# Every fourth column of wo and w2 per result column, and a store of 128 runs of 8 bytes without the turn

## The chip, the core and the metric

The kernel runs on one core of a Trainium2 chip. Its engines are TensorE (PE; PEld is its loading of weights), VectorE (DVE), ScalarE (ACT), GpSimd (POOL) and SyncE (SP), with 16 DMA engines. SBUF is the on-chip memory with 128 partitions, PSUM the memory that TensorE writes to. The metric is device time in microseconds (us), the median of several executions.

## What is computed

One token goes through two branches, which a gate mixes:

```
q = x @ wq                                  # 32 heads of 128
p = softmax(q . k * 128**-0.5)              # each head over 4096 cached keys
a = concat(p . v) @ wo                      # 4096 -> 512
b = relu(x @ w1 + b1)**2 @ w2 + b2          # 512 -> 1376 -> 512
g = sigmoid(sum(x * gate_w))
out = g * a + (1 - g) * b                   # 512 values, bf16
```

All inputs are bf16. The caches of keys and values are 32 MB each; wq and wo are 4 MB each, w1 and w2 1.4 MB each. Every byte is used once.

## The kernel before

**Stages.** The 32 heads are worked in 8 groups of 4 (`NQ`, `R`). For each group a block of keys (K, 4 MB) and of values (V, 4 MB) is loaded. Part of the key scores is computed on DVE (L680, L684), the rest by turning keys on TensorE (L455), copying them on ACT (L350) and multiplying (L462). Then come the softmax (L367 on ACT) and the product with V (`pv`, L492 and L496). The engines run side by side and hand over by semaphores; TensorE's program is a loop written with branches.

**The order of the loads** is written out by hand (`ORDER`, L59): SP issues wq, then K and V blocks, each after the block that held its buffer is done (`done`, L243). w1 is issued behind the third block, once `s_z` and `s_b2` are up (L268, L269). wo comes in four parts of 1 MB; a part goes out when the earlier one in its buffer has been used (`s_wd`, L254). w2 comes last, in five pieces (`W2_PARTS`, L65): 4, 4, the rest of 96 rows, 1 and 1 blocks of 128 rows. Small inputs are loaded on ACT's queue at the start: x, gate_w, b1 and b2 (L321 to L324).

**The output sum.** `acc` is 128 partitions by 4 columns of fp32 in PSUM. It takes all products of both branches: `out_rows` (L524) adds 32 products for each of four groups of rows of wo, `mlp_out` (L533) 4 products for each block of w2. In column j, `acc` holds the values 128j to 128j + 127, since the weights of a product are 128 consecutive columns of wo or w2. The bias b2 is brought to that layout near the start: it is loaded as 4 rows of 128, turned by one transpose on TensorE (L603) into `B2`, and multiplied with 1 - g on DVE (`bias`, L668).

**The end.** TensorE runs `out_rows(1)`, then the five pieces of `mlp_out`, each behind the wait for its load. DVE adds the bias and casts to bf16 (`accs`, L751). TensorE turns the 128 x 4 sum into 4 x 128 (L641), DVE copies it to SBUF (`fin4`, L753), and SP stores it as 4 runs of 256 bytes (L281). SP waits for that store behind a barrier of all engines (L755, L756).

Of the kernel before, what the change touches and what calls it, by code (L numbers as in the profile page):

```python
# [5 lines left out]
def bass_gated_mix__gqa_block_cached__dense_activation_squared_relu__decode_kernel(  # L6
# [16 lines left out]
    bf16 = mybir.dt.bfloat16  # L23
# [6 lines left out]
    DM = 512  # L30
# [49 lines left out]
    with ctx:  # L80
        def sb(name, shape, dt):
            return ctx.enter_context(nc.sbuf_tensor(name, shape, dt))

        def pb(name, shape, dt):
            return ctx.enter_context(nc.psum_tensor(name, shape, dt))

        def sem(name):
            return ctx.enter_context(nc.semaphore(name))
# [5 lines left out]
        wo_sb = W[:, 0:2 * TB * DM].rearrange("p (g t n) -> p g t n", g=2, t=TB)  # L94
# [4 lines left out]
        w1_sb = sb("w1_sb", [128, 4, F], bf16)  # L99
# [7 lines left out]
        xrow = w1_sb[0:1, 0, 0:DM]  # L107
        grow = w1_sb[0:1, 1, 0:DM]
        b1r = sb("b1r", [1, F], bf16)
        b2r = w1_sb[0:4, 2, 0:128]  # L110
        oT = sb("oT", [GH, 128], bf16)
        o2 = sb("o2", [128, TB], bf16)
        fin4 = sb("fin4", [4, 128], bf16)
        zeros = sb("zeros", [128, 128], bf16)
        xb = sb("xb", [128, 4, 128], bf16)
        ident = sb("ident", [128, 128], bf16)
# [19 lines left out]
        hs = sb("hs", [128, FG + 1], bf16)  # L136
        b2g = sb("b2g", [128, 4], fp32)
        accs = sb("accs", [128, 4], bf16)
# [4 lines left out]
        pO = pb("pO", [128, 512], fp32)  # L143
# [6 lines left out]
        OT = KP[2][0:GH, 0:128]  # L150
        O2 = KP[3][:, 0:2 * TB].bitcast(fp32)
        Z = pO[:, 76:77]
        B2 = pO[:, 78:80].bitcast(bf16)
        acc4 = pO[0:4, 128:192].bitcast(bf16)
        QR = [pQ[:, :]] + [p[:, :].bitcast(fp32) for p in KP[0:3]] + [pQ[:, :]] * (NQ - QF)
        H = KP[0][:, 0:2 * (FG + 1)].bitcast(fp32)
        acc = pQ[:, 256:260]
# [3 lines left out]
        s_b = sem("s_b")  # L161
# [20 lines left out]
        s_b2 = sem("s_b2")  # L182
# [27 lines left out]
        s_oc = sem("s_oc")  # L210
        s_acc = sem("s_acc")
        s_as = sem("s_as")
        s_fin = sem("s_fin")
        s_f4 = sem("s_f4")
        s_out = sem("s_out")

        def key(q, b):
# [10 lines left out]
        @block.sync  # L228
        def _(eng):
            def load_kv(n):  # L230
                kind, q = ORDER[n]
                if q >= 2:
                    done(kind, q - 2)
                if kind == "K":
                    eng.dma_start(KV[:, K_SLOT[q], :], k_q[q, :, :]).then_inc(s_k[q], 16)
                else:
                    at = 0
                    for m, sv in zip(V_PARTS[q], s_v[q]):
                        a, b = at * PB * 128, (at + m) * PB * 128
                        eng.dma_start(KV[:, V_SLOT[q], a:b], v_q[q, :, a:b]).then_inc(sv, 16)  # L240
                        at += m

            def done(kind, q):  # L243
                if kind == "K":
                    eng.wait_ge(s_sd, NP * (q + 1))
                    eng.wait_ge(s_t, GQ * (q + 1))
                else:
                    eng.wait_ge(s_pv, q + 1)

            def load_wo(g):  # L250
                if g == 0:
                    eng.wait_ge(s_qps, NQ)
                elif g < NG - 1:
                    eng.wait_ge(s_wd, g)  # L254
                a = 0 if g < NG - 1 else 1
                eng.dma_start(wo_sb[:, a, :, :], wo_v[g, :, :, :]).then_inc(s_wo[a], 16)  # L256

            def load_w2(n):
                a, b = W2_PARTS[n]
                if a < FG:  # L260
                    eng.dma_start(w2a[:, a:b, :], w2_v[:, a:b, :]).then_inc(s_w2[n], 16)  # L261
                else:
                    eng.dma_start(w2b[:, :], B_w2[FG * 128:F, :]).then_inc(s_w2[n], 16)

            for n in range(len(ORDER)):
                load_kv(n)
                if n == 2:
                    eng.wait_ge(s_z, 1)  # L268
                    eng.wait_ge(s_b2, 1)  # L269
                    eng.dma_start(w1_sb[:, :, :], w1_v[:, :, :]).then_inc(s_w1, 16)  # L270
                if n in WO_AT:
                    load_wo(WO_AT[n])
            load_wo(NG - 1)
            eng.wait_ge(s_sd, NP * NQ)
            load_w2(0)
            load_w2(1)
            load_w2(2)
            load_w2(3)
            load_w2(4)
            eng.wait_ge(s_f4, 1)  # L280
            eng.dma_start(out[0, 0, :].rearrange("(j p) -> j p", p=128), fin4[:, :]).then_inc(s_out, 16)  # L281


        @block.gpsimd
# [35 lines left out]
        def _(eng):  # L320
            eng.dma_start(xrow, A_x[0, :, :]).then_inc(s_x, 16)  # L321
            eng.dma_start(grow, gate_w.rearrange("(a n) -> a n", a=1)).then_inc(s_gw, 16)
            eng.dma_start(b1r[:, :], B_b1.rearrange("(a n) -> a n", a=1)).then_inc(s_b, 16)
            eng.dma_start(b2r, B_b2.rearrange("(j p) -> j p", p=128)).then_inc(s_b, 16)  # L324
            eng.wait_ge(s_xc, 1)
            eng.activation(xcolf[:, :], XC, ACT.Copy).then_inc(s_xf, 1)
            eng.wait_ge(s_xf, 1)
# [75 lines left out]
        def _(eng):  # L403
# [45 lines left out]
            def take(sm, n=1):  # L449
                eng.wait_ge(sm, n).then_inc(sm, -n)  # L450
# [73 lines left out]
            def out_rows(a):  # L524
                take(s_oc)
                take(s_wo[a], 16)
                for t in range(TB):
                    for j in range(4):
                        mm = eng.matmul(acc[:, j:j + 1], wo_sb[:, a, t, j * 128:(j + 1) * 128], o2[:, t:t + 1],
                                        start=False, stop=False, skip_group_check=True)  # L530
                mm.then_inc(s_wd, 1)

            def mlp_out(c, last=False):  # L533
                eng.wait_ge(s_w2[c], 16)
                a, b = W2_PARTS[c]
                for n in range(a, b):
                    M = 128 if n < FG else FR
                    w = w2a[:, n, :] if n < FG else w2b[:, :]
                    for j in range(4):
                        mm = eng.matmul(acc[:, j:j + 1], w[:, j * 128:(j + 1) * 128], hs[0:M, n:n + 1],  # L540
                                        start=False, stop=last, skip_group_check=True)
                if last:
                    mm.then_inc(s_acc, 1)
# [33 lines left out]

            at("rows")
            out_rows(0)
            branch("IS_GE", LAST, "next", "rows2")  # L580
            at("rows2")
# [6 lines left out]
            for t in range(4):  # L588
                mm = eng.matmul(XC[:, t:t + 1], xrow[:, t:DM:4], ident[0:1, 0:1], start=True, stop=True)
# [10 lines left out]
            eng.wait_ge(s_qc, QF)  # L600
            eng.wait_ge(s_b, 32)
            eng.wait_ge(s_ez, 1)
            eng.transpose(B2, b2r, ident[0:4, 0:4]).then_inc(s_b2, 1)  # L603

            part("k0")
            keys(0, extra[0])
# [24 lines left out]
            turn()  # L631
            spread()
            out_rows(1)
            eng.wait_ge(s_hs, 2)
            mlp_out(0)
            mlp_out(1)
            mlp_out(2)
            mlp_out(3)
            mlp_out(4, last=True)
            eng.wait_ge(s_as, 1)  # L640
            eng.transpose(acc4, accs[:, :], ident[:, :]).then_inc(s_fin, 1)  # L641


        @block.vector
        def _(eng):
# [20 lines left out]
            def bias():  # L666
                eng.wait_ge(s_b2, 1)
                eng.tensor_scalar(b2g[:, :], B2, omg[:, 0:1], None, ALU.mult).then_inc(s_bg, 1)  # L668

# [79 lines left out]
            eng.wait_ge(s_acc, 1)  # L749
            eng.wait_ge(s_bg, 1)  # L750
            eng.tensor_tensor(accs[:, :], acc[:, 0:4], b2g[:, :], ALU.add).then_inc(s_as, 1)  # L751
            eng.wait_ge(s_fin, 1)
            eng.tensor_copy(fin4[:, :], acc4).then_inc(s_f4, 1)  # L753

        body.close()  # L755
        nc.sync.wait_ge(s_out, 16)  # L756
# [28 lines left out]
```

## Time and profile before

| | |
|---|---|
| median of 3 executions (lowest, highest) | 190.78 us (190.7, 190.9) |
| the profiled execution's own time | 190.89 us |
| its span, first to last instruction | 189.40 us |
| mean granted TensorE clock | 0.732 |
| busy in the span: PE, PEld, DVE, ACT | 73%, 63%, 65%, 61% |
| HBM read | 78.32 MB, 414 GB/s over the span |

The span is cut into 40 slices of 4.7 us; in a row of tenths a 9 means that an engine was busy for 90% or more of the slice. A group of instructions is told by its line, engine and operation, then the tiles (out<-in) and the shapes (partitions x elements). The chain of waits goes back from the last instruction to whatever released it, step by step. SPq is the queue in which SP issues transfers. Times in the views count from the start of the span. The trace also holds records of single DMA packets and of semaphore changes, which the views sum up.

### The profile page before, as it was taken

How to read it: one execution, taken by the hardware profiler on the slowest of the kernel's cores; microseconds unless marked ns; L12 is line 12 of the kernel's file. 1: busy time of each engine (PE TensorE's matmuls, PEld its weight loads, DVE VectorE, ACT ScalarE, POOL GpSimd, SP SyncE). 2: the span in 40 equal slices, each digit the busy share in tenths (PEclk: the TensorE clock that was granted, in tenths of full speed). 3: DMA queues.
4: the chain of work that ended last, by engine and by line, in shares of the span. 5: the costliest groups of instructions: out<-in, count | busy, mean ns of one | idle time of the engine just before them, and what ended most of it. 6: DMA issues, size and time to landing. Idle time of an engine off the chain costs nothing. (4 is left out here: it accounts for less than half of the span.)

```text
span 189.4 us, 6230 instructions
## 1 busy us (share of the span) xinstructions
PE 137.5 (73%) x2685; PEld 119.8 (63%) x2688; DVE 122.7 (65%) x123; ACT 115.7 (61%) x242; POOL 6.0 (3%) x13
## 2 busy tenths in 40 slices
PE   0009496668839889969968797929867496899865
PEld 0003265546729689958858695919666585789854
DVE  1100199979959999996998299919990599701010
ACT  3004559949989985985987099708962298560000
POOL 4000000001600000000000000000000000000000
PEclk9999979979966965795885569555965588555555
DMA  6999999989989999999999999999999999999991
GB/s 225 437 443 443 443 443 439 422 365 484 433 379 438 429 443 439 431 429 429 443 431 401 436 429 436 443 443 429 417 448 408 422 431 434 445 398 410 424 382 68
DMA packets 4177, 78.47 MB, mean 414 GB/s; under 512 B 483, under 2 KB 837, under 8 KB 1094
## 3 DMA queue, kind: packets, MB, share of 16 engines
q1 hardware_dynamic: 4152, 78.32, 97.1%
q8 instruction: 7, 0.11, 0.2%
q14 instruction: 4, 0.03, 0.0%
q10 hardware_dynamic: 14, 0.01, 0.0%
HBM read 78.32 MB, written 0.00 MB: 414 GB/s over the span
## 5 line engine op out<-in xcount | busy, mean ns | idle before, releaser
L350 ACT ACTIVATE kT<-KP 128x1024 bf16<-128x1024 bf16 x80 | 75.2, 1043 | 25.8 <-PE KP L455 25.6
L680 DVE TENSOR_TENSOR w2a<-KV,qb 128x1536 f32<-128x1536 bf16 x32 | 56.1, 1752 | 19.1 <-DMA KV<-in_A_k_cache_dram 18.7
L455 PE MATMUL KP<-ident,KV 128*128 128x128 bf16 x640 | 58.3, 252 | 10.2 <-PEq L450 10.1
L684 DVE TENSOR_REDUCE S<-w2a 128x12 f32<-128x1536 f32 x32 | 56.1, 1753 | 1.1
L455 PEld LDWEIGHTS KP<-ident,KV 128*128 128x128 bf16 x640 | 47.2, 114 | 13.8 <-issue 12.8
L462 PE MATMUL pS<-qc,kT 128*128 128x4 bf16 x640 | 28.0, 165 | 13.2 <-PEq L450 11.2
L462 PEld LDWEIGHTS pS<-qc,kT 128*128 128x128 bf16 x640 | 24.4, 99 | 19.3 <-issue 18.0
L496 PEld LDWEIGHTS pO<-E,KV 128*128 128x128 bf16 x1024 | 29.4, 105 | 0.2 <-issue 0.2
L496 PE MATMUL pO<-E,KV 128*128 128x4 bf16 x1024 | 28.6, 166 | 0.1
L367 ACT ACTIVATE E<-S,nM 32x128 bf16<-32x128 f32 x32 | 18.5, 578 | 0.9
L440 PE MATMUL pQ<-W,xb 128*128 128x512 bf16 x17 | 6.7, 530 | 13.6 <-DMA W<-in_A_wq_dram 12.0
L333 ACT ACTIVATE qb<-pQ 32x128 bf16<-32x128 f32 x20 | 5.3, 268 | 13.9 <-PE pQ L440 13.5
L440 PEld LDWEIGHTS pQ<-W,xb 128*128 128x128 bf16 x20 | 2.2, 126 | 15.1 <-DMA W<-in_A_wq_dram 11.7
L356 ACT ACTIVATE S<-pS 32x80 f32<-32x80 f32 x32 | 7.3, 228 | 4.8 <-PE pS L462 4.2
L659 DVE TENSOR_SCALAR e<-ez 128x1 f32<-128x1 f32 x1 | 0.2, 155 | 13.7 <-ACT ez L382 13.7
L367 ACT ACTIVATION_READ_ACCUMULATOR E<-S,nM 32x1 f32 x32 | 8.1, 252 | 0.0
L703 DVE RECIPROCAL rden<-pO 128x4 f32<-128x4 f32 x8 | 1.4, 174 | 8.4 <-PE pO L496 8.4
L492 PE MATMUL pO<-RS,onesf 128*128 128x4 f32 x16 | 4.3, 340 | 1.4 <-PEq L450 1.4
L483 PE MATMUL pM<-identf,mp 128*1 128x128 f32 x8 | 2.9, 359 | 3.2 <-PEq L450 2.9
L492 PEld LDWEIGHTS pO<-RS,onesf 128*128 128x128 f32 x16 | 3.8, 298 | 1.7 <-issue 1.6
L487 PE MATMUL pM<-onesf,dg 1*128 1x1 f32 x16 | 4.1, 324 | 0.9 <-PEq L450 0.7
L440 PE MATMUL KP<-W,xb 128*128 128x512 bf16 x12 | 4.7, 576 | 0.0
(74 smaller groups left out, 68.9 us busy)
## 6 DMA issues: line engine op xcount, KB each, us to landing
KV<-in_A_k_cache_dram SPq DMA_DIRECT2D x8, 4096.0 KB, 21.9
KV<-in_A_v_cache_dram SPq DMA_DIRECT2D x7, 4096.0 KB, 29.5
W<-in_A_wq_dram SPq DMA_DIRECT2D x1, 4096.0 KB, 13.2
W<-in_A_wo_dram SPq DMA_DIRECT2D x4, 1024.0 KB, 16.7
KV<-in_A_v_cache_dram SPq DMA_DIRECT2D x1, 2048.0 KB, 11.3
KV<-in_A_v_cache_dram SPq DMA_DIRECT2D x2, 1024.0 KB, 14.3
w_sb<-in_B_w_dram SPq DMA_DIRECT2D x1, 1376.0 KB, 24.0
w2a<-in_B_w_dram SPq DMA_DIRECT2D x2, 512.0 KB, 18.8
```

What stands on the lines that cost most here:

```text
L333: eng.activation(qb[rows(r), c, :], QR[c][rows(r), r * 128:(r + 1) * 128], ACT.Copy)\
L350: eng.activation(kT[:, n % NT, :], KP[n % NKP][:, :], ACT.Copy).then_inc(s_ev, 1)
L356: eng.activation(S[rows(r), q % NS, 0:YQ], S2[rows(r), :, r], ACT.Copy).then_inc(s_cp, 1)
L367: eng.activation(E[rows(r), q % 2, :, r], S[rows(r), q % NS, :], ACT.Exp, bias=nM[rows(r), q:q + 1], scale=SCALE, accum_out=RS[rows(r), q ...
L440: mm = eng.matmul(QR[c], xb[:, t, :], wq_sb[:, t, c * 512:(c + 1) * 512], start=(t == 0), stop=(t == 3))
L455: mm = eng.transpose(KP[(GQ * a + g) % NKP][:, y * 128:(y + 1) * 128], key(a, b), ident[:, :])
L462: mm = eng.matmul(pS[:, R * c:R * c + R], kT[:, (GQ * a + g) % NT, y * 128:(y + 1) * 128], qc2[:, a, :], start=True, stop=True)
L487: eng.matmul(MB[:, a:a + 1], dg[:, a, :], onesf[0:1, 0:1], start=True, stop=True).then_inc(s_mb, 1)
L492: eng.matmul(DEN[a], onesf[:, :], RS[:, a, :], start=True, stop=True)
L496: mm = eng.matmul(O[a], KV[:, V_SLOT[a], b * 128:(b + 1) * 128], E[:, a, COLUMN[b], :], start=(b == 0), stop=(b == NB - 1))
L680: eng.tensor_tensor(prod, KV[:, K_SLOT[q], x:x + XB * 128].rearrange("p (b d) -> p b d", d=128), qb[:, q, :].unsqueeze(1).to_broadcast([12 ...
L684: eng.tensor_reduce(S[:, q % NS, c:c + XB], prod, AX.X, ALU.add).then_inc(s_sd, 1)
```

## The change

The weights of a product are no longer 128 consecutive columns but every fourth one, beginning at j. So column j of `acc` holds the values j, j + 4, j + 8 and so on, and partition p holds the four consecutive values 4p to 4p + 3. The turn (L641) and the copy (L753) are gone, with `fin4` and two semaphores. SP waits for the add and stores `accs` straight away, as 128 runs of 8 bytes. The bias follows the same layout: b2 is loaded as one row of 512, and four products with a 1 x 1 one, each reading every fourth element, put it into four fp32 columns of PSUM.

```diff
-        b2r = w1_sb[0:4, 2, 0:128]
+        b2r = w1_sb[0:1, 2, 0:DM]
...
-        B2 = pO[:, 78:80].bitcast(bf16)
-        acc4 = pO[0:4, 128:192].bitcast(bf16)
+        B2 = pO[:, 78:82]
...
-            eng.wait_ge(s_f4, 1)
-            eng.dma_start(out[0, 0, :].rearrange("(j p) -> j p", p=128), fin4[:, :]).then_inc(s_out, 16)
+            eng.wait_ge(s_as, 1)
+            eng.dma_start(out[0, 0, :].rearrange("(p j) -> p j", j=4), accs[:, :]).then_inc(s_out, 16)
...
-            eng.dma_start(b2r, B_b2.rearrange("(j p) -> j p", p=128)).then_inc(s_b, 16)
+            eng.dma_start(b2r, B_b2.rearrange("(a n) -> a n", a=1)).then_inc(s_b, 16)
...
-                        mm = eng.matmul(acc[:, j:j + 1], wo_sb[:, a, t, j * 128:(j + 1) * 128], o2[:, t:t + 1],
+                        mm = eng.matmul(acc[:, j:j + 1], wo_sb[:, a, t, j:DM:4], o2[:, t:t + 1],
...
-                        mm = eng.matmul(acc[:, j:j + 1], w[:, j * 128:(j + 1) * 128], hs[0:M, n:n + 1],
+                        mm = eng.matmul(acc[:, j:j + 1], w[:, j:DM:4], hs[0:M, n:n + 1],
...
-            eng.transpose(B2, b2r, ident[0:4, 0:4]).then_inc(s_b2, 1)
+            for j in range(4):
+                mm = eng.matmul(B2[:, j:j + 1], b2r[:, j:DM:4], ident[0:1, 0:1], start=True, stop=True)
+            mm.then_inc(s_b2, 1)
...
-            eng.wait_ge(s_as, 1)
-            eng.transpose(acc4, accs[:, :], ident[:, :]).then_inc(s_fin, 1)
...
-            eng.wait_ge(s_fin, 1)
-            eng.tensor_copy(fin4[:, :], acc4).then_inc(s_f4, 1)
```

More of the change, by code (lines that the diff above doesn't have):

```diff
@@ L109, in bass_gated_mix__gqa_block_cached__dense_activation_squared_relu__decode_kernel @@
         b1r = sb("b1r", [1, F], bf16)
-        b2r = w1_sb[0:4, 2, 0:128]
+        b2r = w1_sb[0:1, 2, 0:DM]
         oT = sb("oT", [GH, 128], bf16)
         o2 = sb("o2", [128, TB], bf16)
-        fin4 = sb("fin4", [4, 128], bf16)
         zeros = sb("zeros", [128, 128], bf16)
@@ L212, in bass_gated_mix__gqa_block_cached__dense_activation_squared_relu__decode_kernel @@
         s_as = sem("s_as")
-        s_fin = sem("s_fin")
-        s_f4 = sem("s_f4")
         s_out = sem("s_out")
```

## The prediction

> **What bounds the kernel now.** The page first: its second part shows the DMA engines full in nearly every slice, its third part puts the loading queue at 97.1% of them, and the weight loads of TensorE at 63%.
>
> ```profile
> DMA  6999999989989999999999999999999999999991
> ...
> q1 hardware_dynamic: 4152, 78.32, 97.1%
> ```
>
> So the 78 MB of loads set the time until they are in, and what the change does to compute before that matters only where compute holds back a load. After the last load comes a short tail in which nothing overlaps. The chain of waits, in order of time, shows both:
>
> ```profile
> 167.12 19.15 DMA w2a<-in_B_w_dram
> 186.26 0.05 issue
> 186.31 0.80 PE pQ L540 x24
> 187.11 0.03 issue
> 187.14 0.28 PE pQ L540 x4
> 187.42 0.02 issue
> 187.45 0.17 DVE accs L751
> 187.62 0.04 issue
> 187.66 0.28 PE pO L641
> 187.95 0.02 issue
> 187.97 0.21 DVE fin L753
> ```
>
> The reader is to see that the loads of w2 end at 186.3, and that then single instructions follow each other: the last w2 products, the add of the bias, the turn (L641), the copy (L753), and the store, which the chain no longer lists. The span ends at 189.40. One more thing is in the trace's semaphore records: the fifth piece of w2 lands at 187.09, so the last four products (187.14) wait for their own load, not for the 24 before them.
>
> The timeline of the last microseconds gives the store, and how densely products with consecutive columns stand:
>
> ```profile
> 185.34 0.50 PEld L540 LDWEIGHTS pQ<-hs,w2a 128*128 128x128 bf16 x16
> ...
> 188.21 0.33 SPq L281 DMA_DIRECT2D out_dram<-fin  x1
> ```
>
> Sixteen weight loads of 104 ns in 0.50 us: (0.50 - 0.104) / 15 = 26 to 27 ns from one to the next. I call this the step; it sets the rate of these products, each of which lasts 165 ns but overlaps the others.
>
> **What is removed.** The turn and the copy with their hand-overs. The add's semaphore is up at 187.620, the copy's at 188.193 (semaphore records), and SP issues 16 ns after it. SP would issue 16 ns after the add instead: 188.193 - 187.620 = **0.573 us** earlier. All of it lies on the path. In the built program of the changed kernel the store does wait for the add alone, so nothing else takes the place of the two. What is late next is the store itself; the engines' closing barrier is passed by 188.98, before the store's landing at 189.37, and moves with the issue.
>
> **Strided weights in the tail.** 76 products read every fourth column now: 32 of the last out_rows, 16 of the first piece of w2, 24 of the pieces two to four, and the last 4. Elements 8 bytes apart are loaded in one place of the trace (L589, one row, clock 1.00), elements 20 bytes apart in another (L508, clock 0.50; the last 4 of its 44 are consecutive):
>
> ```profile
> L589 PEld LDWEIGHTS pO<-ident,w_sb x4: 105/110/114, 2.1 to 2.2; 1*128 1x128 bf16 x4
> ...
> L508 PEld LDWEIGHTS KP<-xcol,w_sb x44: 136/157/196, 167.4 to 172.4; 128*128 128x128 bf16 x40, 128*96 128x96 bf16 x4
> ```
>
> L589's four fill 0.21 us, so its step is (0.21 - 0.11) / 3 = 32 ns against 27: 5 ns more. L508's starts stand 58 ns apart: 31 ns more. What hides it: the first 48 products start at 184.48 and the last of them starts at 185.74 (its load 185.739), while the second piece is waited for until 186.30, which leaves 0.54 us, or 11 ns each. The next 24 have until 187.14 instead of 186.95: 0.19 us, or 8 ns each. Only the last 4 pay whatever it is. At 32 ns a step that is 4 x 5 = 0.02 us. L589 ran at twice the clock of the tail; if its 5 ns become 10, the 24 overrun by 0.05 and the four add 0.04, together 0.09. I take **0.05**, between the two, because L589 has the same distance of bytes; the ends are 0 and, by L508's step, 76 x 58.5 = 4.45 us from 184.48, so a last step ending at 188.92 instead of 187.25: 1.68 us. A gain is excluded: the columns are no fewer.
>
> The Trainium skill (SBUF — State Buffer, "Door 1: The DMA port swizzle") says that memory is read at full rate as long as two accesses fall into one 16-byte line. By it the 8 bytes cost nothing and the sum below is 190.51 instead of 190.56; L508 at 20 bytes agrees with its other half, and no run here shows it at 128 rows and 8 bytes.
>
> **Strided weights earlier.** Three calls of out_rows (32 products each) become 0.16 us longer at 5 ns, 1.0 us at 31 ns. SP waits for them (L256) before it issues the next wo and the V behind it on its queue. The loads already issued cover that: the page has 21.9 us (K) and 29.5 us (V) from issue to landing, while 4096 KB at 443 GB/s need 9.5 us, so over 10 us are always queued. I cost it at nothing; without the cover it would be 0.16 us a call. At L603 four products replace one: 3 x 32 ns = 0.1 us later for s_b2. SP's wait there (L269) holds the load of w1, which lands 24.0 us after issue at 22.79 and is used at 167; TensorE itself then sits idle for 1.2 us until K0 is in (23.8). Nothing. The load of b2 as one run instead of four leaves the same queue before 2.1 us and is waited for at 22.4. The bias product (L668, 213 ns) reads fp32 now, like L751 (161 ns); it lies at 42.9, beside loads.
>
> **The store.** Now: 4 runs of 256 bytes. The packet records show issue at 188.209, packets on four DMA engines starting at 188.966 to 189.026 and taking 15 to 18 ns, and the last landing at 189.369, 0.32 us after the last packet. Then: 128 runs of 8 bytes. Packets of 8 bytes take 7 ns (one is in the trace) and the 4-byte ones after the store's data begin 12 ns behind them, so eight on an engine are some 8 x 12 = 0.10 us, 0.09 more than now. The only issue of 128 rows that met idle engines is the first (L223): issued at 0.740, it began on ten engines from 1.747 to 1.897, 17 ns apart, on four more until 2.292, on the last two at 2.706 and 2.780. At 17 ns sixteen engines begin within 15 x 17 = 0.25 us, 0.19 more than the store's 0.06 now. So +0.28; I take **0.30**, since ten of sixteen engines go that way. The ends: no cost (a gain of at most the 0.06 of spread), and the two late engines, (2.780 - 0.740) - (189.026 - 188.209) = 1.22, with the packets 1.31. SP's own 334 ns do not change: issues with 128 rows take 328.
>
> **The sum.** -0.573 + 0.05 + 0.30 = -0.22 us. The profiled execution took 190.89 (span 189.40 and 1.49 around it): 190.67. It lies 0.11 over the median 190.78, and against that the forecast is **190.56 us**. About 0.2% (0.38 us) is what a measurement of this kernel can tell from no change, so faster begins below 190.40 and slower above 191.16.
>
> **The rivals.**
>
> *The store costs almost nothing more.* If sixteen engines begin as close together as four do and the packets hide, it costs 0.05, the weights 0.02: -0.50, **190.28**. For it: the issue takes SP the same time, and the receipt (0.32 us) is the larger part. Against it: L223's spread. The Trainium skill (DMA: Bandwidth & Descriptors, "Anatomy of one DMA") holds that many descriptors can be emitted before their cost shows, which is this case. Chance 0.27.
>
> *Two engines begin late, as at L223*: -0.573 + 0.05 + 1.31 = +0.79, **191.57**. Against it: these were the kernel's first packets, and the two did it once. Chance 0.10.
>
> *The weight loads become the bound.* If 8 bytes cost what 20 do, TensorE is late by 1.68 us: -0.573 + 1.68 + 0.30 = +1.41, **192.19**. The place is the tail from 184.48 on; with the store at +0.30 the change loses once the last product is over 0.27 us late, at (187.25 + 0.27 - 184.48) / 76 = 40 ns a step, against 27 now, 32 at L589 and 58 at L508. For it: those 58 are the only strided loads with 128 rows. Against it: L589. Chance 0.08.
>
> *The short writes go one after the other*: if each of an engine's eight waited for a receipt of 0.32 us, seven more cost 2.25: -0.573 + 0.05 + 0.19 + 2.25 = +1.92, **192.70**. No packet of the trace waits so. The Trainium skill (same page, "Specifications") says that writes below 512 bytes are read, modified and written; the present 256 bytes are below it too and show no such time. Chance 0.06.
>
> **How the numbers follow.** The forecast has 0.49 (190.40 to 191.16, the store between 0.15 and 0.9). Faster 0.27 is the first rival, slower 0.10 + 0.08 + 0.06 = 0.24. The range reaches from the full 0.573, 190.2, over the late engines, 191.6; the last two rivals, 0.14, stay outside.
>
> **What would show it.** After the change the store should be issued at about 187.69, with the add 0.2 us ahead of it and neither turn nor copy between. The steps of L540 (x16) and of L529 should be 27 to 37 ns; at 40 or more the weights decide. The last four products should still start at about 187.14, set by their load. From the issue to the span's end it is 1.19 us now (188.21 to 189.40): 1.25 is the first rival, 1.5 the forecast, 2.5 late engines. The forecast is wrong if a wait of SP or a dip of the DMA row appears earlier, since all of the middle is costed at nothing.

## The result

The changed kernel takes 192.26 us (192.14 to 192.6), the kernel before beside it 190.84: a ratio of 1.0075 with an interval of 1.0063 to 1.0087, so +1.42 us. Forecast were 190.56 us, a small gain, and a range that ended at 191.6. The profiled execution took 192.17 us, with a span of 190.87.

The page of the changed kernel has the DMA engines as full as before, up to the last slice but one:

```profile
DMA  6999999989999999999999999999999999999980
...
q1 hardware_dynamic: 4288, 78.32, 96.4%
```

The last packet of the loads ends at 186.79 us, 0.12 later than the 186.68 of before; what is new lies behind it. The chain of waits of the changed kernel:

```profile
184.68 0.04 issue
184.72 1.20 PE pQ L525 x32
185.92 1.65 PE pQ L536 x44
187.57 0.02 issue
187.59 0.16 DVE accs L747
```

The turn and the copy are gone, and the chain now runs through the products from 184.7 on, not through a load of w2. The waits for loads are only shorter, not gone: by the semaphore records the second piece of w2 lands at 186.376 and its first weight load starts at 186.418, and the fifth lands at 187.212 with its first weight load at 187.255. The chain stops with the add at 187.75 and leaves the store out; the span ends at 190.87. The timeline of the changed kernel shows the products and the store's issue:

```profile
185.75 1.27 PEld L536 LDWEIGHTS pQ<-hs,w2a 128*128 128x128 bf16 x32
...
187.59 0.16 DVE L747 TENSOR_TENSOR accs<-pQ,b2g 128x4 bf16<-128x4 f32 x1 [3.17 <-PE pQ L536]
187.78 0.35 SPq L277 DMA_DIRECT2D out_dram<-accs  x1
```

The store is issued at 187.78, 0.43 us earlier than the 188.21 of before. What is new comes after that. SP's waits, first before, then after (line waited at, total us, times, longest):

```profile
SPq L756 <- DMA out_dram<-fin: 0.4, 1, 0.4
```

```profile
SPq L750 <- DMA out_dram<-accs: 2.4, 1, 2.4
```

And the stretches of the changed kernel after the loads (busy time of the engines, clock, DMA share, GB/s):

```profile
187.80:188.60 0.80, 0.00 (x0) 0.00 (x0) 0.00 (x0) 0.00 (x0) 0.00 (x0) 0.50 0.00 0
188.60:188.83 0.23, 0.00 (x0) 0.00 (x0) 0.00 (x0) 0.00 (x0) 0.00 (x0) 0.50 0.34 5
188.83:190.90 2.07, 0.00 (x0) 0.00 (x0) 0.00 (x0) 0.00 (x0) 0.00 (x0) 0.50 0.00 0
```

The reader is to see that the store's packets move in 0.2 us (188.60 to 188.83) and that then, for 2.07 us, nothing works at all: no engine, no DMA engine. The kernel waits for the landing of packets that have left. In the trace's records the two stores compare like this (us):

| | before | after | difference |
|---|---|---|---|
| store issued | 188.209 | 187.782 | -0.427 |
| issue to first packet | 0.757 | 0.841 | +0.084 |
| first packet to end of last | 0.081 | 0.203 | +0.122 |
| end of last packet to last landing | 0.322 | 2.010 | +1.688 |
| last landing to end of span | 0.032 | 0.033 | +0.001 |
| span | 189.401 | 190.869 | +1.468 |

The sixteen DMA engines' landings do not come together. The first is at 189.02, 0.2 us after the last packet, and the others follow up to 190.84.

### The profile page after: what moved, and what is told of

It reads as the page before. It is cut to its first block, busy times and chain, and to the rows that moved or that the text cites. A ratio compares the mean times of both kernels' runs of the same rounds, so it can differ in the third digit from the quotient of the medians.

```text
span 190.9 us, 6236 instructions
## 1 busy us (share of the span) xinstructions
PE 138.4 (73%) x2690; PEld 121.9 (64%) x2690; DVE 122.8 (64%) x122; ACT 116.0 (61%) x242; POOL 6.0 (3%) x13
## 5 line engine op out<-in xcount | busy, mean ns | idle before, releaser
L451 PE MATMUL KP<-ident,KV 128*128 128x128 bf16 x640 | 60.1, 257 | 10.3 <-PEq L446 10.3
L451 PEld LDWEIGHTS KP<-ident,KV 128*128 128x128 bf16 x640 | 49.0, 117 | 13.5 <-issue 12.4
L458 PEld LDWEIGHTS pS<-qc,kT 128*128 128x128 bf16 x640 | 24.9, 100 | 18.5 <-issue 17.1
L436 PE MATMUL pQ<-W,xb 128*128 128x512 bf16 x20 | 7.8, 531 | 12.6 <-DMA W<-in_A_wq_dram 11.5
L525 PE MATMUL pQ<-o,W 128*128 128x1 bf16 x128 | 4.8, 172 | 0.5 <-PEq L446 0.5
L525 PEld LDWEIGHTS pQ<-o,W 128*128 128x128 bf16 x128 | 4.6, 117 | 0.6 <-issue 0.6
```

The source lines that it names most:

```text
L436: mm = eng.matmul(QR[c], xb[:, t, :], wq_sb[:, t, c * 512:(c + 1) * 512], start=(t == 0), stop=(t == 3))
L451: mm = eng.transpose(KP[(GQ * a + g) % NKP][:, y * 128:(y + 1) * 128], key(a, b), ident[:, :])
L458: mm = eng.matmul(pS[:, R * c:R * c + R], kT[:, (GQ * a + g) % NT, y * 128:(y + 1) * 128], qc2[:, a, :], start=True, stop=True)
L525: mm = eng.matmul(acc[:, j:j + 1], wo_sb[:, a, t, j:DM:4], o2[:, t:t + 1], start=False, stop=False, skip_group_check=True)
```

## The experiments

The theory after the result: the store alone costs it all, through its landing. The rivals: the strided weights (the forecast's rival of 192.19 us had nearly the measured time); that sixteen engines' landings come one after another by themselves; and that every short write costs 14 ns wherever it lies (the 1.81 us from the first landing to the last, over 127). Against these stands that writes wait for each other only where several fall into the same few bytes of memory.

**The store without the weights.** The kernel before, with the changed end:

```diff
-            eng.wait_ge(s_as, 1)
-            eng.transpose(acc4, accs[:, :], ident[:, :]).then_inc(s_fin, 1)
...
-            eng.dma_start(out[0, 0, :].rearrange("(j p) -> j p", p=128), fin4[:, :]).then_inc(s_out, 16)
+            eng.dma_start(out[0, 0, :].rearrange("(p j) -> p j", j=4), accs[:, :]).then_inc(s_out, 16)
```

> The kernel before with the change's end alone: consecutive weight columns, no turn, no copy, accs stored as 128 runs of 8 bytes (so the values stand in another order in out). If the store is the cause (its 16 receipts came from 0.20 to 2.01 us after the last packet of 8 bytes began): +1.2 to +1.5 us against before, with the receipts again spread over 1.5 us or more. If the strided weights are the cause: -0.3 us, the 0.573 us of the turn and the copy less 0.3 for the store.

Measured: ratio 1.0039 (1.0025 to 1.0053), +0.74 us by the ratio and +0.82 by the medians, less than the +1.2 expected; the last landing 2.83 us after issue, the sixteen spread over 1.6 us. So the store costs, the sign is settled, but the size fell short of the whole change.

**The weights without the store.** The changed kernel with the end of before:

```diff
             mlp_out(4, last=True)
+            eng.wait_ge(s_as, 1)
+            eng.transpose(acc4, accs[:, :], ident[:, :]).then_inc(s_fin, 1)
...
-            eng.dma_start(out[0, 0, :].rearrange("(p j) -> p j", j=4), accs[:, :]).then_inc(s_out, 16)
+            eng.dma_start(out[0, 0, :].rearrange("(j p) -> j p", p=128), fin4[:, :]).then_inc(s_out, 16)
```

> The changed kernel with the end of before: strided columns of wo and w2 and the new bias, but with the turn, the copy and the store of 4 runs of 256 bytes (so the values stand in another order in out). If the store is the cause: 0 to +0.15 us against before, with a step of 33 ns between weight loads, the last store issued some 0.6 us after the add and landed 1.2 us after its issue. If the strided weights are the cause: +1.4 us or more.

Measured: ratio 0.9998 (0.9988 to 1.0008). From its timeline:

```profile
184.47 1.12 PEld L529 LDWEIGHTS pQ<-o,W 128*128 128x128 bf16 x32 [0.56 <-issue]
...
186.31 0.61 PEld L540 LDWEIGHTS pQ<-hs,w2a 128*128 128x128 bf16 x16 [0.19 <-DMA w2a<-in_B_w_dram]
...
187.48 0.16 DVE L753 TENSOR_TENSOR accs<-pQ,b2g 128x4 bf16<-128x4 f32 x1 [3.27 <-PE pQ L540]
...
188.24 0.33 SPq L281 DMA_DIRECT2D out_dram<-fin  x1
```

Thirty-two weight loads of 117 ns in 1.12 us are a step of (1.12 - 0.117) / 31 = 32 ns against 27. The second piece of w2 is still waited for at 186.31, and the add starts 0.03 us later than before (187.45). The rival of the weights is out.

**Do the two parts add up?** The whole change and the store alone again:

> The changed kernel once more, because the change as a whole cost 1.42 us and its store alone 0.8 us with weights that alone cost nothing. If the two parts add up: +0.8 to +1.0 us against before, and the first figure was high by the luck of the receipts. If they do not: +1.4 us again, and something joins them.

> The store alone once more, beside the whole change on the same chip. If the two parts add up: within 0.15 us of the whole change. If the weights cost something only together with this store: 0.3 to 0.6 us below it again.

> The changed kernel on the same chip as the store alone: +1.2 to +1.4 us against before, with receipts of the store anew spread over 1.3 us or more.

Measured: the whole change 1.0064 (1.0046 to 1.0082) and 1.0055 (1.0042 to 1.0068); the store alone, on the same chip as the latter, 1.0073 (1.0049 to 1.0097). By the medians the whole change costs +1.19 us, between its two branches, and then +1.07, a little under the range expected. The store alone has the same median as the latter, 191.99 us. So on the chip where both ran they add up; that the store alone cost only +0.82 in its first run is not explained. The last landings came 2.64 to 3.10 us after issue in the five profiled executions of the whole change and of the store alone, 1.16 before, so part of the change's size is that spread.

**Fewer, longer runs on all sixteen engines.**

```diff
-            eng.dma_start(out[0, 0, :].rearrange("(p j) -> p j", j=4), accs[:, :]).then_inc(s_out, 16)
+            eng.dma_start(out[0, 0, :].rearrange("(p j) -> p j", j=32), zeros[0:16, 0:32]).then_inc(s_out, 16)
```

> The changed kernel, but the last store takes 16 runs of 64 bytes of zeros, one for each DMA engine, instead of the sum (the sum is computed and not stored). If the receipts of sixteen engines come one after another by themselves, about 0.11 us each: landing again 3 us after issue, time as after the change. If it is the number of short writes (128 of them at 14 ns each), or that several short writes go to the same line of the memory: landing about 1.3 to 1.5 us after issue and 1.6 to 1.8 us less than after the change, so about 0.3 us below before.

Measured: 190.63 us in one execution, fifteen of the landings 1.16 to 1.34 us after issue and one at 1.64. Sixteen engines by themselves are not it.

**The same runs, far apart.**

```diff
+        far = nc.dram_tensor("far", [128, 256], bf16, kind="Internal").ap()
...
-            eng.dma_start(out[0, 0, :].rearrange("(p j) -> p j", j=4), accs[:, :]).then_inc(s_out, 16)
+            eng.dma_start(far[:, 0:4], accs[:, :]).then_inc(s_out, 16)
```

> The changed kernel with the same 128 runs of 8 bytes, but each 512 bytes from the next in a scratch tensor (out gets zeros at the start, so the sum is not in it). If every short write costs 14 ns wherever it lies: landing 3 us after issue as after the change. If the writes wait for each other because they share a line of the memory: landing about 1.4 us after issue, receipts within 0.3 us of each other. If it is the engines: 3 us.

Measured: all sixteen landings 1.23 to 1.39 us after issue, 190.41 us in one execution. SP's wait for the landing is 0.7 us, where the changed kernel has 2.4:

```profile
SPq L755 <- DMA far<-accs: 0.7, 1, 0.7
```

The same engines, the same 128 packets of 8 bytes, the same source; only the addresses differ. That the scratch tensor is another one than out does not matter: without gaps, such a store to a scratch tensor takes 3.27 us (below). So it is not the number of short writes either. Timed:

> The run with 128 runs of 8 bytes 512 bytes apart once more, timed (out gets zeros at the start, the sum is in the scratch tensor). If runs that share a line are the whole cost: -0.3 us against before (0.573 less 0.23 for the later landing after issue, less up to 0.1 for the weights). If something else of the change costs too: 0 or more.

Measured: 1.0014 (0.9997 to 1.0030), with ten executions between 190.34 and 192.19. That is no gain, against the expectation. In the profiled one the last packet of the loads ended 0.36 us later than before (187.04 against 186.68) and one landing came at 2.00 us, fifteen by 1.39. This kernel also stores zeros at its start, ahead of the K loads on SP, but the record does not bear out that this moves the loads: the same kernel, profiled in the run ahead, ended them at 186.69 and had a span of 189.11 us, 0.29 less than before, and the changed kernel, which has no such store, ended them at 187.01 on the chip of this run. The one late landing may go with a fetch of instructions (16 KB) that ended just as the store's packets began: the other store with a single late landing, the 16 runs of 64 bytes, had such a fetch end 0.3 us ahead of its packets, and the run ahead had none there. That was not tested. This run leaves open what the change would be worth if its writes did not meet, not what they cost where they do.

**How near is near.** The changed kernel, and behind its store one store after another, each waiting for the one ahead:

```diff
+            eng.wait_ge(s_out, 16)
+            eng.dma_start(far0[:, 0:4], accs[0:128, :]).then_inc(s_out, 16)
+            eng.wait_ge(s_out, 32)
+            eng.dma_start(far1[:, 0:4], accs[0:128, :]).then_inc(s_out, 16)
...
```

> The changed kernel, and behind its store eight more to scratch tensors, one at a time: 128 runs of 8 bytes, 8, 16, 32, 64, 128, 256, 512 and again 8 bytes from one run to the next. If short writes wait for each other in a line of the memory: some 2.8 to 3.1 us from issue to landing at 8 bytes, falling to 1.4 us where a line holds only one run (at 64 bytes if the line is 64). If the cost hangs on the size of the touched area instead: a gradual fall up to 512. The added stores lengthen the time by about 16 us, which means nothing.

SP's timeline of that kernel; each issue waits for the landing ahead, so the distance between two lines is the upper one's time from issue to landing. The first is the store of out, then 8, 16, 32, 64, 128, 256, 512 and 8 bytes from run to run:

```profile
187.73 0.35 SPq L285 DMA_DIRECT2D out_dram<-accs  x1
191.16 0.33 SPq L287 DMA_DIRECT2D far<-accs  x1
194.43 0.32 SPq L289 DMA_DIRECT2D far<-accs  x1
196.02 0.32 SPq L291 DMA_DIRECT2D far<-accs  x1
197.66 0.32 SPq L293 DMA_DIRECT2D far<-accs  x1
199.06 0.32 SPq L295 DMA_DIRECT2D far<-accs  x1
200.46 0.32 SPq L297 DMA_DIRECT2D far<-accs  x1
201.85 0.32 SPq L299 DMA_DIRECT2D far<-accs  x1
203.26 0.32 SPq L301 DMA_DIRECT2D far<-accs  x1
```

Without gaps 3.27 us (L287 to L289), 1.59 at 16 bytes, 1.64 at 32, and 1.40, 1.40, 1.39 and 1.41 from 64 on. The last, again without gaps, lands 3.06 us after issue (semaphore records). The cost is there when the runs lie 8 bytes apart, most of it is gone at 16 bytes, and all of it at 64; there is no gradual fall up to 512.

> The changed kernel, and behind its store seven more to scratch tensors, one at a time: 128 runs of 4, 8, 16, 32, 64, 128 and 256 bytes without gaps. If runs that share a line wait for each other: about 3 us at 4 and 8 bytes, less at 16 and 32, and 1.4 to 1.5 us from the length on where a run fills a line (64 bytes, if the line is 64). If it is only the number of writes: 3 us at every length.

The runs without gaps, 4, 8, 16, 32, 64 and 128 bytes long from the second line on (the 256 bytes after them landed in 1.43):

```profile
190.56 0.33 SPq L286 DMA_DIRECT2D far<-zeros  x1
198.38 0.32 SPq L288 DMA_DIRECT2D far<-accs  x1
201.13 0.32 SPq L290 DMA_DIRECT2D far<-zeros  x1
203.46 0.32 SPq L292 DMA_DIRECT2D far<-zeros  x1
204.87 0.32 SPq L294 DMA_DIRECT2D far<-zeros  x1
206.27 0.32 SPq L296 DMA_DIRECT2D far<-zeros  x1
207.69 0.32 SPq L298 DMA_DIRECT2D far<-zeros  x1
```

L286, the 4-byte runs, takes 7.82 us for half the bytes of out; 8 bytes 2.75, 16 bytes 2.33, and from 32 bytes on 1.40 to 1.42. The expected limit of 64 was one step too high: a run of 32 bytes pays nothing, with 128 of them on sixteen engines. Sharing 32 bytes is not enough by itself: two runs of 8 bytes share them at a distance of 16 bytes and land at 1.59 us, two touching runs of 16 bytes share them too and land at 2.33.

> The changed kernel, and behind its store eight more to scratch tensors, one at a time: 16, 32, 64 and 113 runs of 8 bytes without gaps (113 has no divisor up to 16 but 1, so that one DMA engine may take them all, which the packets will show), 113 runs 512 bytes apart, 16 runs 64 bytes apart, 4 runs of 256 bytes and 16 runs of 64 bytes. If it is engines that meet in a line: 16, 32 and 64 runs land later the more runs there are, and 113 on one engine land about as soon as 113 that lie apart. If short writes to a line wait for each other whoever sends them: the 113 without gaps land over 1 us later than the 113 apart.

Landings after issue, from the semaphore records: 16 runs of 8 bytes without gaps 1.29 us, 32 runs 3.29, 64 runs 3.62. The 113 runs did go to one engine (114 packets in a row, the last over 1.42 us after issue): 4.17 us without gaps, 2.38 when 512 bytes apart. In SP's timeline the first two lines are these two stores, and the third is the next one:

```profile
199.19 0.27 SPq L293 DMA_DIRECT2D far<-accs  x1
203.38 0.22 SPq L295 DMA_DIRECT2D far<-accs  x1
205.78 0.31 SPq L297 DMA_DIRECT2D far<-accs  x1
```

Sixteen runs 64 bytes apart 1.27, 4 of 256 bytes 1.12, 16 of 64 bytes 1.28. So neither branch holds as it was put: more runs do land later, but the engines need not meet for it. One engine alone is enough for the cost (4.17 against 2.38), and sixteen engines with one run each do not pay it, although their runs touch. In these stores it begins with a second run on an engine. In the 32 runs the late landings come 0.43 to 0.45 us apart (1.27, 1.70, 2.13, 2.58) and the last two 0.70 later (3.28, 3.29), as if each waited for an earlier one; that is a guess from the steps. Which write waits for which, and why 32 runs are as late as 128, stays open.

**Another turn.** Since the weights cost nothing and the store must keep long runs, only the turn was left to shorten. DVE writes the sum into 4 of 32 columns and turns it by itself:

```diff
-            eng.wait_ge(s_fin, 1)
-            eng.tensor_copy(fin4[:, :], acc4).then_inc(s_f4, 1)
+            eng.wait_ge(s_as, 2)
+            for b in range(4):
+                eng.transpose(fin32[:, b * 32:(b + 1) * 32], acc32[b * 32:(b + 1) * 32, :]).then_inc(s_f4, 1)
```

> The kernel before with another turn: DVE writes the sum into the first 4 of 32 columns, turns four blocks of 32 x 32 itself, and SP stores the same 4 runs of 256 bytes. If the whole gain in reach is the hand-over between engines: add to issue 0.4 to 0.5 us instead of 0.589 from the add's end, landing 1.16 us after issue as before, so -0.1 us against before, near what can be told. If the four turns are slow (each as long as the copy, 0.21 us, one after the other): +0.3 us.

Measured: 1.0016 (1.0008 to 1.0025), or +0.30 us by the medians, as expected for slow turns. Its timeline:

```profile
187.73 0.16 DVE L749 TENSOR_TENSOR acc<-pQ,b2g 128x4 bf16<-128x4 f32 x1 [3.22 <-PE pQ L539]
187.93 0.89 DVE L752 STREAM_TRANSPOSE fin<-acc 32x32 bf16<-32x32 bf16 x4
188.85 0.33 SPq L280 DMA_DIRECT2D out_dram<-fin  x1
```

Four turns in a row take 0.89 us, 0.2 each, where the turn on TensorE and one copy need 0.573 with both hand-overs. None of the versions tried was shown to be faster than the kernel before.

## Why the prediction was wrong, point by point

- **What bounds the kernel** was right: loads to 186.8, and a bare tail behind them in which every delay counts in full. The 186.3 that it reads as the end of the w2 loads is the landing of their second piece alone (186.26); in the kernel before the last packet ends at 186.68 and the fifth piece lands at 187.09.
- **What is removed**, 0.573 us: right. The add's semaphore comes at 187.766 and the issue 16 ns later.
- **Strided weights in the tail**, 0.05: right within what can be told (ratio 0.9998 alone), and its working too: a step of 32 to 33 ns, forecast 27 to 37, the 48 and the 24 products under their loads, the last four 0.03 late. (The 32 ns read from L589 was rough: its sum gives 33, and the four starts lie 28 to 32 ns apart.) In the changed kernel's profile the add is 0.15 late, of which 0.12 is that the last piece of w2 landed later (187.21 against 187.09). By the Trainium skill (SBUF — State Buffer, "Door 1: The DMA port swizzle") columns 8 bytes apart cost nothing; the trace does not agree, with some 6 ns more a load (33 against 27), of which the time feels only those 0.03 us.
- **What was costed at nothing in the middle** was nothing: the page's DMA row shows no new dip, and the run of the weights without the store, which has the same middle, ends its loads at 186.68 us, as before.
- **The store** is the step that failed: "I take 0.30", with ends of 0 and 1.31. It measured 0.084 + 0.122 + 1.688 = 1.89 us in the profiled execution. That is 1.59 more than forecast, and with the add 0.10 later than forecast it makes the 1.69 us between the -0.22 expected and the +1.47 of the spans. From issue to the end of the span it is 3.09 us, past the 2.5 named for late engines. The packets were not it: they take 0.122 more, where 0.09 and a spread of 0.19 were forecast, and the first one comes 0.084 later, for which there was no term. The 0.32 us from the last packet to the landing were carried over from the store of 256-byte runs without a bound of their own, and that is where 1.69 us of the 1.89 came from: behind the last packet the changed kernel waits 2.01 us, because its runs of 8 bytes touch (the same runs 512 bytes apart land 1.39 us after issue, against 3.05). The row was a landing of long runs, and nothing in the trace of before showed short runs that touch. A carried-over figure is an unknown cost too, and the range should have been as open there as at the packets.
- **The rivals.** The one whose time fits best (192.19, the weights) is the wrong one, as the step of 33 ns shows; that its time nearly came out is luck. The one with the right place, short writes that wait for a receipt, had a chance of 0.06 on the ground that "No packet of the trace waits so." The packets do not wait; the landings do. Its price was made from seven further waits in a row on each engine and came out at 2.25; the spread of the landings is 1.4 to 1.9, so its mechanism is not the measured one either. The Trainium skill (DMA: Bandwidth & Descriptors, "Specifications") says that writes below 512 bytes are read, modified and written. The traces do not show whether the writes here are; most of the extra time they show is in touching runs of 4, 8 and 16 bytes, and touching runs of 32, 64, 128 and 256 bytes have none. The first rival took the receipt for the larger part. In the kernel before it is not (0.322 of 1.160 us from issue to landing); in the changed kernel it is (2.010 of 3.054), and it is what grew. The Trainium skill (DMA: Bandwidth & Descriptors, "Anatomy of one DMA") has a fixed cost that is mostly the receipt and does not grow with the number of descriptors, but for transfers issued by GpSimd, while SP issues this store; for SP's stores here the cost is not fixed, since 128 descriptors land in 1.4 us or in 7.8.

## What to carry to other kernels

A transfer's time has three parts, issue to first packet, the packets, and the last packet to the landing; take each from the records, and do not carry the third from a transfer whose runs are of another length. Before turning a final store into many runs, look at how long a run is in memory and whether the runs touch: 128 runs of 8 bytes side by side landed 1.2 to 2.0 us later than 128 of 32 bytes. When a forecast's rival has the measured time, check its mechanism by its own row before believing it.

## What the runs showed that was not expected

- Touching runs of 4 bytes landed 7.8 us after issue, of 8 bytes 2.6 to 3.4, of 16 bytes 2.3, of 32 to 256 bytes 1.4; 8-byte runs 64 bytes or more apart 1.4 in five stores and 2.0 in one, with a single late landing. Other lengths than 8 bytes were stored once each.
- A store on all sixteen DMA engines meets whatever else they carry. In four executions a fetch of instructions (16 KB, 0.9 to 1.2 us) began 0.73 to 1.14 us after the issue of the store of out, and the last of the store's packets ended 1.79 to 2.09 us after issue instead of 1.04. The last landing came 2.98 to 3.42 us after issue in these four and 2.64 to 3.05 in the four without; a store without gaps to a scratch tensor took 3.25 with no fetch beside it, so the landings do not show clearly what the fetch costs.
- Weight loads with 128 rows: a step of 27 ns for neighbouring bf16 columns, 33 ns for every fourth, 58 ns for every tenth, at a clock of 0.50.
